# An S4 convolution and SwiGLU block on one core: the front's list of steps written anew, with all its loads in it

## The chip, the core and the metric

The kernel runs on one core of a Trainium2 chip. A core has a matrix engine (TensorE, PE in the profile), a vector engine (VectorE, DVE), a scalar engine (ScalarE, ACT) that evaluates functions from loadable tables, a general engine (GpSimd, POOL), and a sync engine (SyncE, SP) that does nothing but issue DMA transfers. Each engine works through its own instructions in order and waits on semaphores for the others. PE reads from SBUF and writes to PSUM; DMA moves data between DRAM and SBUF. The metric is the device time of one execution in microseconds (us), as the median of several runs.

## The reference

The input `x` has 2048 rows of 640 channels. A conditioning vector `c` gives six modulation rows. The first half is an S4 long convolution, the second a SwiGLU feed-forward net:

```python
mod = (silu(c) @ w_mod).reshape(1, 6, 1, 640)       # sa, ca, ga, sb, cb, gb
h = layernorm(x) * (1 + ca) + sa
dt = exp(log_dt)[:, None]
P = exp((dt * A)[:, :, None] * arange(2048))        # A, B, C complex, 640 x 128
K = einsum("dn,dnl,dn->dl", C, P, dt * B).real      # 640 x 2048
y = irfft(rfft(pad(h)) * rfft(pad(K)))[:2048] + h * Dskip
x = x + ga * y
h = layernorm(x) * (1 + cb) + sb
x = x + gb * ((silu(h @ w1) * (h @ w3)) @ w2)       # w1, w3: 640 x 1728
```

## The kernel before

The kernel has four stretches. The **front** makes everything that the convolution needs to start: the modulation, the normalized input after a first transform stage, and the first part of the convolution's kernel `K`. A **loop** then runs the convolution in five chunks of 128 channels (`NDC`), while it goes on making `K`. A short part turns the result back, and the feed-forward net with its matrix products takes the rest. Only the front, and the first steps of the loop, are touched here.

`K` is made in 40 steps of 16 channels (`NS`, `SD`). For a step, PE multiplies small tables into exponents (`exp_fast`, `exp_slow`: words `PA`, `PQ`), ScalarE takes `Exp` of them (`XA`, `XQ`), POOL makes integer phases in two instructions (`phases`, word `PH`: the product of turns and a ramp, then the addition of a shift to half of it), ScalarE takes the absolute value, cosine and sine of them (`AB`, `CO`, `SI`), VectorE multiplies (`E1`, `E2`, `A1`, `A2`), PE sums products to `pk` (`kg`), VectorE adds and scales (`K`), PE does a first transform stage (`pt`) and ScalarE copies the result into the buffer `uk` (`uk`). `Exp` on one side, and the sine and arctangent on the other, are in different tables, so a change between them costs an `ACT_TABLE_LOAD`.

The front runs the first nine to twelve of these steps, mixed with the rest of its work:

- Parameters: `prm` holds A, B, C, loaded for the first 128 channels (`d0`) and for the other 512 (`d1`). Words `z1` to `zK` turn the first part into the tables that `PA`, `PQ` and `PH` read (`thi` and `phi` are what `PH` reads); words `d0` to `dN` do so for the other 512 channels. `d0` stands on POOL, `d1` on VectorE.
- Modulation: eight column blocks of `w_mod` early (`ms+0` to `ms+7`) and five late (`qs+0` to `qs+4`), each a group of PE matmuls, a VectorE copy (`mp`, `qp`), a PE transposition (`mc`, `qc`) and a VectorE copy into columns (`mv`, `qv`). Five blocks lie in the rooms `wm`, three (`wg`) come into rooms that the first blocks leave, and the five late ones (`wl`) into rooms in `uk` that the parameters leave.
- Input: 16 tiles of 128 rows are loaded (`xl`), measured (`ls`, `lg`, `lv`) and normalized (`ln`). `s1` to `s4` make a row and a `shift` from the modulation. Per tile PE does the first transform stage (`um`), VectorE or ScalarE evicts the two halves with the shift (`ua`, `ub`; `/s` means by ScalarE), and `us` stores the tile to DRAM. `ul` loads that result back, in another layout, into `uk`; four such loads of two DMAs each for a chunk.

Words such as `PA+0/A/3` stand in one long string, `FRONT`. The program walks it from left to right and emits each word's instructions, and every engine keeps the order of its own. The number behind a slash is a count of idle matmuls (`warm`, a product of the identity with itself) that PE does ahead of the word; each is two matmuls in the profile. Some loads of the front stood outside the string: once the words `ms+0`, `ms+1`, `ms+2` were out, a piece of code behind the loop issued the three `wg` blocks, three input tiles and the second part of `prm`, all on SP's queue. When the string ends, the pools `hpz` and `pm_` on the right of SBUF are closed and the pool `fp` opens in their place. `fp` holds the matrices of the second transform stage (`s2`, three buffers) and of the inverse (`i1`).

The first step of the loop is `stage2` for chunk 0 and group 0 (L655 in the profile, `p<-uk,s`): 16 matmuls that need the first `s2` matrices, `ul+0` in `uk` and the front's last `uk` copy. ScalarE's copy `kc` of its result opens VectorE's products.

Of the kernel before, what the change touches and what calls it, by code (L numbers as in the profile page):

```python
# [108 lines left out]
def tile_kernel(ctx: ExitStack, tc: tile.TileContext, a):  # L109
# [248 lines left out]
    pmod, part = {}, {}  # L358

# [17 lines left out]
    def early_sums(i, n):  # L377
        pm = psS.tile([P, 512], F32, name="pm", tag=("pb", "pk")[i % 2 if i < 5 else (i - 5) % 2], bufs=1)
        warm(pm, n)
        mod_sums(i, (wm + wg)[i], pm)  # L380
# [178 lines left out]

    def phases(s):  # L560
        sl = slice(s * SD, s * SD + SD)
        p = tp.tile([P, SD, NPH], I32, name="ph", bufs=4)
        keep(G.tensor_tensor(p, bc(thi[:, sl], 2, NPH), bc(iota, 1, SD), op=OP.mult))  # L563
        keep(G.tensor_tensor(p[:, :, :NA], p[:, :, :NA], bc(phi[:, sl], 2, NA), op=OP.add))  # L564
        ph[s] = p
# [77 lines left out]

    def stage2(ch, g):
        s2 = fp.tile([P, 4, P], F32, name="s2", bufs=3)
        nc.sync.dma_start(s2, a["s2"][:, g * 4:g * 4 + 4, :])
# [176 lines left out]
    def of(p, name, *args):  # L823
        return lambda *n: getattr(p, name)(*args, *n)

    once_parts = {
        "r2": lambda: Vo.tensor_tensor(r2, bc(selx, 2, NB), bc(stepx[:, :NB], 1, NA), op=OP.mult),
# [21 lines left out]
        "xl": ln1_load, "us": u_store, "wl": late_load, "ul": lambda i: u_load(0, i),  # L849
# [39 lines left out]
    for word in FRONT:  # L889
# [739 lines left out]
```

## Time and profile before

| what | value |
|---|---|
| median of 3 runs | 964.46 us (963.45 to 967.33) |
| profiled execution | 967.25 us |
| its span, first to last instruction | 965.5 us |
| mean granted TensorE clock | 0.986 |
| PE busy over the span | 900.3 us (93%) |
| VectorE busy | 709.2 us (73%) |
| ScalarE busy | 560.9 us (58%) |
| POOL busy | 280.9 us (29%) |
| first matmul of the loop (`stage2`) | 153.72 us after the span's start |

Rows of a timeline give start, duration, engine, line, operation, the tiles written and read, and in brackets the engine's idle time before it with what ended that. Rows of stretches give the busy time of PE, PE's weight loads, VectorE, ScalarE and POOL in turn, each with its count of instructions, and then the granted PE clock, the busy share of the DMA engines and GB/s. Nearly all calls in the front go through one recording helper, so their line is L103 for PE and VectorE and L137 or L140 for ScalarE, and the tile's name tells them apart. "SPq" is SP's issuing of DMAs.

### The profile page before, as it was taken

How to read it: one execution, taken by the hardware profiler on the slowest of the kernel's cores; microseconds unless marked ns; L12 is line 12 of the kernel's file. 1: busy time of each engine (PE TensorE's matmuls, PEld its weight loads, DVE VectorE, ACT ScalarE, POOL GpSimd, SP SyncE). 2: the span in 40 equal slices, each digit the busy share in tenths (PEclk: the TensorE clock that was granted, in tenths of full speed). 3: DMA queues.
4: the chain of work that ended last, by engine and by line, in shares of the span. 5: the costliest groups of instructions: out<-in, count | busy, mean ns of one | idle time of the engine just before them, and what ended most of it. 6: DMA issues, size and time to landing. Idle time of an engine off the chain costs nothing.

```text
span 965.5 us, 21228 instructions
## 1 busy us (share of the span) xinstructions
PE 900.3 (93%) x8524; PEld 706.3 (73%) x8524; DVE 709.2 (73%) x1249; ACT 560.9 (58%) x815; POOL 280.9 (29%) x278
## 2 busy tenths in 40 slices
PE   4899996888888899899999999999999999999997
PEld 3676674666666676568888887777888888888886
DVE  6688975999999995677666665686887766664665
ACT  4778986999999964255433333365743333323432
POOL 2623452545564621224322210111422222200000
PEclk8999999999999999799999999999999999999999
DMA  8545598555566799593313114995422221103452
GB/s 250 165 165 192 193 269 203 141 158 134 148 165 160 186 220 277 158 277 130 84 53 109 56 55 116 244 254 178 142 91 82 77 60 52 52 21 98 147 170 103
DMA packets 103720, 140.79 MB, mean 146 GB/s; under 512 B 20581, under 2 KB 62821, under 8 KB 103621
## 3 DMA queue, kind: packets, MB, share of 16 engines
q1 hardware_dynamic: 99812, 129.34, 46.7%
q0 software_dynamic: 2304, 7.74, 2.4%
q10 hardware_dynamic: 1504, 2.36, 0.8%
q8 instruction: 67, 1.10, 0.5%
q14 instruction: 33, 0.26, 0.1%
HBM read 107.94 MB, written 31.46 MB: 144 GB/s over the span
## 4 chain that ended last, share of the span: by engine, by line
PE 80%; ACT 8%; DVE 4%; DMA 3%; issue 3%; SPq 0%; ACTq 0%; POOL 0%; DVEq 0%; POOLq 0%
PE ps L103 56%; PE p L655 6%; PE pu L103 3%; ACT A L137 3%; PE pk L605 3%; PE pt L624 3%; PE pm L103 3%; PE pz L697 2%; ACT cs L137 2%; DMA zs<-zt 2%; PE pa L537 1%; PE pq L548 1%; PE pa L103 1%; PE pT L103 1%; ACT uk L140 1%
## 5 line engine op out<-in xcount | busy, mean ns | idle before, releaser
L103 DVE TENSOR_TENSOR s<-ps,s 128x512 f32<-128x512 f32 x138 | 94.9, 687 | 79.9 <-PE ps L103 79.7
L563 POOL TENSOR_TENSOR ph<-thi,iota 128x1024 int32<-128x1024 int32 x40 | 95.0, 2376 | 138.4 <-DVE A L591 69.5
L103 DVE TENSOR_TENSOR gl<-rw,gh 128x640 fp32r<-128x640 f32 x87 | 78.2, 898 | 64.9 <-ACT gh L103 64.8
L103 ACT CAST gh<-rw 128x640 fp32r<-128x640 f32 x87 | 63.3, 727 | 104.0 <-PE ps L103 62.2
L655 PE MATMUL p<-uk,s 128*64 128x256 f32 x640 | 79.7, 391 | 19.1 <-issue 9.9
L103 PE MATMUL ps<-xA,gh 128*128 128x512 f32 x280 | 87.9, 392 | 0.4 <-ACT xA L103 0.4
L103 PE MATMUL ps<-gh,uh 128*128 128x512 f32 x224 | 87.5, 391 | 0.0
L103 POOL TENSOR_TENSOR S<-rw 128x256 f32<-128x256 f32 x46 | 36.6, 798 | 174.0 <-DVE S0l L103 154.7
L103 PE MATMUL ps<-gl,uh 128*128 128x512 f32 x224 | 87.2, 389 | 0.0
L103 PE MATMUL ps<-gh,ul 128*128 128x512 f32 x208 | 81.1, 390 | 0.0
L655 PEld LDWEIGHTS p<-uk,s 128*64 128x64 f32 x640 | 46.1, 139 | 42.3 <-issue 14.3
L584 DVE TENSOR_TENSOR E<-A,cs 128x1024 f32<-128x1024 f32 x40 | 60.3, 1509 | 1.7 <-ACT cs L137 1.7
L103 PEld LDWEIGHTS ps<-xA,gh 128*128 128x128 f32 x280 | 52.1, 188 | 13.0 <-ACT xA L103 1.0
L103 PE MATMUL ps<-xA,gl 128*128 128x512 f32 x140 | 54.5, 389 | 0.0
L564 POOL TENSOR_TENSOR ph<-ph,phi 128x512 int32<-128x512 int32 x40 | 49.5, 1236 | 6.5 <-DVE phi L103 3.5
L591 DVE TENSOR_TENSOR A<-A,ph 128x1024 f32<-128x1024 f32 x40 | 50.4, 1260 | 0.0
L103 ACT ACTIVATE s<-ps 128x512 f32<-128x512 f32 (+1 forms) x33 | 19.6, 595 | 51.3 <-PE ps L103 51.3
L103 PEld LDWEIGHTS ps<-gl,uh 128*128 128x128 f32 x224 | 42.1, 188 | 9.0
L103 PEld LDWEIGHTS ps<-gh,uh 128*128 128x128 f32 x224 | 42.0, 188 | 8.8
L697 PEld LDWEIGHTS pz<-Y,i 64*128 64x128 f32 x640 | 39.4, 188 | 11.1 <-issue 5.8
L697 PE MATMUL pz<-Y,i 64*128 64x128 f32 x640 | 44.4, 282 | 3.2 <-issue 2.7
L137 ACT ACTIVATE A<-pa 128x1024 f32<-128x1024 f32 x40 | 41.1, 1029 | 8.5 <-PE pa L537 8.2
(241 smaller groups left out, 2318.3 us busy)
## 6 DMA issues: line engine op xcount, KB each, us to landing
rw<-in_w_dram SPq DMA_DIRECT2D x52, 320.0 KB
us<-u SPq DMA_DIRECT2D x16, 640.0 KB
s<-in_s_dram SPq DMA_DIRECT2D x40, 256.0 KB
i<-in_i_dram SPq DMA_DIRECT2D x40, 256.0 KB
rw<-in_wg_dram SPq DMA_DIRECT2D x31, 320.0 KB
rw<-in_wu_dram SPq DMA_DIRECT2D x28, 320.0 KB
uk<-us SPq DMA_DIRECT2D x32, 256.0 KB
zs<-zt SPq DMA_DIRECT2D x32, 256.0 KB
```

Source lines behind the costliest of these rows:

```text
L103: ins = fn(*args, **kw)
L137: return tc.keep_in_program_order(S.activation(*args, **kw))
L140: return tc.keep_in_program_order(S.copy(out, in_))
L537: keep(PE.matmul(pA[s][:, rr, :], la[r, t, :], r2[r, js, :].rearrange("p j b -> p (j b)"), start=True, stop=True, tile_position=(r.start, 0)))
L563: keep(G.tensor_tensor(p, bc(thi[:, sl], 2, NPH), bc(iota, 1, SD), op=OP.mult))
L564: keep(G.tensor_tensor(p[:, :, :NA], p[:, :, :NA], bc(phi[:, sl], 2, NA), op=OP.add))
L584: keep(V.tensor_tensor(EC[s][:, :, 1:3, :], AA[s][:, :, 1:3, :], mid(cs[s]), op=OP.mult))
L591: keep(V.tensor_tensor(A[:, :, 1:3, :], A[:, :, 1:3, :], mid(ph[s]), op=OP.mult))
L605: keep(PE.matmul(pk[dq * 32:dq * 32 + 32, g, :], x[:, g * 4 + dq, 1, :], x[:, g * 4 + dq, 0:3:2, :], start=(st == 0), stop=(st == 1), tile ...
L624: keep(PE.matmul(pt[c * 64:c * 64 + 64, g, :], kk[:, g, :], s1[:, c, :], start=True, stop=True, tile_position=(0, c * 64)))
L655: keep(PE.matmul(p2[par * 64:par * 64 + 64, pi, c, :], s2[:, pi * 2 + par, c * 64:c * 64 + 64], uk[:, 0:kn + 1:kn, f, :], start=True, stop ...
L697: ins = keep(PE.matmul(pz[:, par, (g % 2) * 2 + pi, :], i1[r, pi, c, :], Y[r, pi, c, :], start=(c == 0), stop=(c == 1), tile_position=(par ...
```

## The change

Five things are done:

- The loads that the code behind the loop issued become words of the string: `wg+0` to `wg+2`, `pd` (the second part of `prm`) and `xl+4` to `xl+6`.
- `PH` is split: `PH` keeps the product, and a new word `PI` does the addition of the shift.
- In the pool `pm_` the tiles `lt` and `scb` change their places, so that what lies at the place of the first `s2` buffers is something else.
- The words `ul+1` to `ul+3` leave the string. Behind it the first three `s2` loads are issued at once, in program order, and then the three `ul` loads. `stage2` takes these three `s2` tiles instead of loading its own.
- The string is written in another order, with other counts of idle matmuls (117 in all, where there were 205) and another division of the evictions (17 by ScalarE, where there were 16). ScalarE's order has 19 table loads up to its first `kc`, where it had 18.

```diff
@@ pool pm_
-    scb = pm_.tile([P, KD, NA], F32, name="scb")
     rrow = pm_.tile([P, D], F32, name="rrow")
     shift = pm_.tile([P, D // 2], F32, name="shift")
+    lt = pm_.tile([P, 2, D - DC], F32, name="lt")
+    scb = pm_.tile([P, KD, NA], F32, name="scb")
     cols = pm_.tile([P, 7, KD], F32, name="cols")
-    lt = pm_.tile([P, 2, D - DC], F32, name="lt")
@@ modulation
+    wg = {}
+    def gate_load(i):
+        n = (256, 256, 128)[i]
+        wg[i] = w_load(w_room(1, i, n, 1280), 1280 + 256 * i)
@@ phases
+    def phase_turns(s):
+        p = ph[s] = tp.tile([P, SD, NPH], I32, name="ph", bufs=4)
+        keep(G.tensor_tensor(p, bc(thi[:, s * SD:s * SD + SD], 2, NPH), bc(iota, 1, SD), op=OP.mult))
+    def phase_shift(s):
+        p = ph[s]
+        keep(G.tensor_tensor(p[:, :, :NA], p[:, :, :NA], bc(phi[:, s * SD:s * SD + SD], 2, NA), op=OP.add))
@@ second stage
+    def s2_load(g):
+        s2 = fp.tile([P, 4, P], F32, name="s2", bufs=3)
+        (Qo if len(s2_first) < 3 else nc.sync).dma_start(s2, a["s2"][:, g * 4:g * 4 + 4, :])
+        s2_first.append(s2)
+        return s2
     def stage2(ch, g):
-        s2 = fp.tile([P, 4, P], F32, name="s2", bufs=3)
-        nc.sync.dma_start(s2, a["s2"][:, g * 4:g * 4 + 4, :])
+        s2 = s2_load(g) if ch or g >= 3 else s2_first[g]
@@ once_parts
+        "pd": lambda: Qo.dma_start(prm[:, :, d1], prma[:, :, d1]),
@@ FRONT, its first words
-        "r2 z1 x0 z2 z3 ld2 sc zF sel zG ms+0/1 z4 z6 z5 zB zJ z7 zH r1 zC mp+0 ms+1/1 zI z8 z9/4 mp+1 mc+0 "
+        "r1 r2 x0 sel sc ms+0 z5 z1 z7 z8 xl+4 z2 z9 ld2 z3 ms+1 mp+0 zA zF mc+0 z4 zG zJ PA+0/A/3 z6 mp+1 "
...
@@ the walk through FRONT
-        if not wg and {"ms+0", "ms+1", "ms+2"} <= emitted:
-            wg = [w_load(w_room(1, i, c, 1280), 1280 + 256 * i) for i, c in enumerate((256, 256, 128))]
-            for j in range(4, 7):
-                ln1_load(j)
-            Qo.dma_start(prm[:, :, d1], prma[:, :, d1])
-    in_order[0] = False
     pre.close()
     fp = ssm.enter_context(tc.tile_pool(name="fp", bufs=2, side="right", reuse_waits="tile"))
+    for g in range(3):
+        s2_load(g)
+    for i in range(1, 4):
+        u_load(0, i)
+    in_order[0] = False
```

**SP at the front's end.** Here stand the last late blocks of `w_mod`, the last store `us`, the loads of `uk` from `us` (`ul`), the `s2` and `i1` matrices, before:

```order
L103 DMA us_57<-u_1449 128x1280
L103 DMA uk_82<-in_w_mod_dram 128x5x288
L103 DMA uk_82<-in_w_mod_dram 128x5x96
L103 DMA uk_82<-in_w_mod_dram 128x5x384
L103 DMA uk_82<-us_57 64x8x128 x8
L646 DMA s2_1820<-in_s2_dram 128x512
L646 DMA s2_1889<-in_s2_dram 128x512
L646 DMA s2_1999<-in_s2_dram 128x512
L688 DMA i1_2043<-in_i1_dram 128x512
L688 DMA i1_2158<-in_i1_dram 128x512
L688 DMA i1_2215<-in_i1_dram 128x512
```

and now:

```order
L103 DMA uk_82<-in_w_mod_dram 128x5x384
L103 DMA us_57<-u_1340 128x1280
L103 DMA uk_82<-us_57 64x8x128 x2
L103 DMA s2_1728<-in_s2_dram 128x512
L103 DMA s2_1730<-in_s2_dram 128x512
L103 DMA s2_1732<-in_s2_dram 128x512
L103 DMA uk_82<-us_57 64x8x128 x6
L651 DMA uk_82<-us_57 64x8x128 x2
L705 DMA i1_1959<-in_i1_dram 128x512
L658 DMA s2_2018<-in_s2_dram 128x512
L705 DMA i1_2074<-in_i1_dram 128x512
L658 DMA s2_2110<-in_s2_dram 128x512
```

The first three `s2` loads now stand behind two `uk` loads instead of eight. The last `us` store has moved behind all late blocks of `w_mod`. The first `i1` load has moved behind the two loads for chunk 1, which wait for the second `stage2`.

**SP early on.** Behind the constants and the first four input tiles stood:

```order
L103 DMA uk_82<-in_w_mod_dram 128x5x160
L103 DMA uk_82<-in_w_mod_dram 128x5x96
L103 DMA uk_82<-in_w_mod_dram 128x5x256
L103 DMA uk_82<-in_w_mod_dram 128x5x128
L103 DMA x_286<-in_x_dram 128x640
L103 DMA x_288<-in_x_dram 128x640
L103 DMA x_290<-in_x_dram 128x640
L103 DMA uk_82<-in_prm_dram 128x6x512
```

and now:

```order
L103 DMA x_170<-in_x_dram 128x640
L103 DMA uk_82<-in_w_mod_dram 128x5x160
L103 DMA uk_82<-in_w_mod_dram 128x5x96
L103 DMA uk_82<-in_prm_dram 128x6x512
L103 DMA x_240<-in_x_dram 128x640
L103 DMA uk_82<-in_w_mod_dram 128x5x256
L103 DMA x_345<-in_x_dram 128x640
L103 DMA x_433<-in_x_dram 128x640
L103 DMA uk_82<-in_w_mod_dram 128x5x128
```

The large `prm` load has moved ahead of the second and third `wg` blocks, each of which waits until PE has left its room.

**VectorE ahead of the shift.** `cols` are the modulation's columns; the five instructions with `cols` on both sides are `s1`, whose result PE turns into the row from which the shift is made. Ahead of them stood:

```order
L103 COPY part_351<-pm_342 128x256
L584 TENSOR_TENSOR E_366<-A_242,cs_248 128x16x64
L587 TENSOR_TENSOR E_366<-A_242,cs_248 128x16x32
L103 SCALAR_TENSOR_TENSOR rs1_229<-mv1_228,rs1_229 128x2
L103 COPY part_387<-pm_353 128x256
L103 COPY cols_105<-pm_353 128x2
L103 SCALAR_TENSOR_TENSOR rs1_304<-mv1_303,rs1_304 128x2
L591 TENSOR_TENSOR A_242<-A_242,ph_223 128x16x64
L595 SCALAR_TENSOR_TENSOR A_242<-ph_223,A_242 128x16x32
L103 COPY cols_105<-pm_342 128x2
L103 TENSOR_SCALAR cols_105<-cols_105 128x5 x2
```

and now:

```order
L103 BN_STATS st1_265<-x_136 128x6 x2
L103 BN_AGGR mv1_266<-st1_265 128x2
L103 COPY part_322<-pm_253 128x256
L103 COPY part_326<-pm_307 128x256
L103 BN_STATS st1_328<-x_170 128x6 x2
L103 BN_AGGR mv1_329<-st1_328 128x2
L103 COPY cols_106<-pm_307 128x2
L103 COPY cols_106<-pm_253 128x2
L103 TENSOR_SCALAR cols_106<-cols_106 128x5 x2
```

The four products of step 0 (`E` and `A`) have moved from ahead of `s1` to behind it, and the statistics of a fifth input tile have come ahead of it.

More of the change, by code (lines that the diff above doesn't have):

```diff
@@ L379, in early_sums @@
         warm(pm, n)
-        mod_sums(i, (wm + wg)[i], pm)
+        mod_sums(i, wm[i] if i < 5 else wg[i - 5], pm)
     def early_turn(i):
@@ L558, in slow @@
             pQ.pop(s)[:, :, :256].rearrange("p r (j b) -> p r j b", j=8), AF.Exp)
-    def phases(s):
[L561 to L565, printed above, removed]
+    def phase_turns(s):
[4 more added lines that the diff above has]
+        keep(G.tensor_tensor(p[:, :, :NA], p[:, :, :NA], bc(phi[:, s * SD:s * SD + SD], 2, NA), op=OP.add))
+    def phases(s):
+        phase_turns(s)
+        phase_shift(s)
     def absph(s):
@@ L848, in tile_kernel @@
         "qs": late_sums, "qp": lambda i: mod_part(("l", i)), "qc": late_turn, "qv": late_cols,
[L849 removed]
+        "xl": ln1_load, "us": u_store, "wl": late_load, "wg": gate_load, "ul": lambda i: u_load(0, i),
         "ls": ln_sums, "lg": ln_power, "lv": ln_bias, "ln": ln_apply}
@@ L908, in tile_kernel @@
                 done.add((name, k))
-                if name == "PA":
+                if name == "PH":
+                    phase_turns(k)
+                elif name == "PI":
+                    phase_shift(k)
+                elif name == "PA":
                     exp_fast((k,), tag, n)
```

2 lines of the change are left out of this document (1 added, 1 removed), and 45 rows, old and new, of the table FRONT.

## The prediction

> **What bounds the kernel now.** I read first, in the view of the timeline, how the front hands over to the loop, since the change ends there.
>
> ```profile
> 134.34 11.50 SPq L103 DMA_DIRECT2D uk<-us  x8
> 145.88 2.59 SPq L646 DMA_DIRECT2D s<-in_s_dram  x3
> 148.57 1.62 SPq L688 DMA_DIRECT2D i<-in_i_dram  x3
> 147.85 1.09 PE L624 MATMUL pt<-s,K 128*64 128x128 f32 x16
> 148.99 0.58 ACT L140 COPY uk<-pt 128x512 f32<-128x512 f32 x1 [0.17 <-PE pt L624]
> 153.72 3.56 PE L655 MATMUL p<-uk,s 128*64 128x256 f32 x16 [4.78 <-issue]
> 157.31 0.59 ACT L140 COPY kc<-p 128x512 f32<-128x512 f32 x1 [6.78 <-PE p L655]
> 160.25 1.95 PE L655 MATMUL p<-uk,s 128*64 128x256 f32 x16 [0.91 <-PE pt L624]
> 172.10 1.05 PE L697 MATMUL pz<-Y,i 64*128 64x128 f32 x16
> ```
>
> The first second-stage group could start when ScalarE's last `uk` copy is done, at 148.99 + 0.58 = 149.57. It starts at 153.72. The profile gives "issue" as the reason, which names no engine; what that group still needs is data, and its matrices `s` were issued last, at 145.88, behind eight `uk` loads that kept SP's queue for 11.50 us. PE then runs this group in 3.56 us where the next takes 1.95. ScalarE, whose `kc` copy opens the loop, stands idle for 6.78 us. So the front's end holds about 6 us in which no engine gets on.
>
> Next I read the front in five stretches (busy time of PE, weight loads, VectorE, ScalarE, POOL; clock; DMA share; GB/s).
>
> ```profile
> 0.00:38.00 38.00, 25.19 (x210) 20.61 (x212) 21.73 (x65) 22.90 (x31) 13.95 (x17) 0.91 0.87 263
> 38.00:52.00 14.00, 9.90 (x98) 8.08 (x99) 10.71 (x16) 10.38 (x14) 7.70 (x5) 0.88 0.00 0
> 52.00:75.00 23.00, 22.38 (x313) 17.37 (x313) 20.61 (x36) 17.39 (x24) 9.03 (x14) 1.00 0.53 188
> 75.00:110.00 35.00, 33.52 (x567) 24.39 (x570) 32.16 (x73) 32.02 (x40) 11.48 (x13) 1.00 0.52 189
> 110.00:150.00 40.00, 37.79 (x689) 28.81 (x688) 30.54 (x49) 35.15 (x41) 22.02 (x12) 1.00 0.89 246
> ```
>
> PE looks busiest, but much of that is idle matmuls (below). From 75 to 150 ScalarE works 67.17 of 75 us and is the bound. Ahead of that it is idle 15.10, 3.62 and 5.61 us, 24.3 of 75. The DMA engines rest completely from 38 to 52. Those two facts are what another order can use; the sum is made on ScalarE.
>
> The reasons for the early idle time are in the timeline from 4 to 56 us:
>
> ```profile
> 18.48 9.17 SPq L103 DMA_DIRECT2D uk<-in_w_mod_dram  x4
> 19.29 0.89 DVE L103 BATCH_NORM_STATS2 st<-x 128x6 f32<-128x320 f32 x2 [0.38 <-DMA x<-in_x_dram]
> 20.39 1.02 ACT L137 ACTIVATE A<-pa 128x1024 f32<-128x1024 f32 x1 [0.55 <-PE pa L537]
> 27.25 0.42 DVE L103 COPY part<-pm 128x256 f32<-128x256 f32 x1 [5.81 <-PE pm L103]
> 29.37 0.38 SPq L103 DMA_DIRECT2D uk<-in_prm_dram  x1
> 37.67 4.80 POOL L103 TENSOR_TENSOR uk<-uk 128x512 f32<-128x512 f32 x3 [6.72 <-DMA uk<-in_prm_dram]
> 40.09 1.25 DVE L103 TENSOR_SCALAR cols<-cols 128x5 f32<-128x5 f32 x2
> 44.40 2.50 PE L103 MATMUL pr<-ident,cols 128*128 128x128 f32 x10 [4.10 <-DVE cols L103]
> 46.94 1.06 ACT L137 ACTIVATE shift<-pr,misc 64x320 f32<-64x320 f32 x2 [3.18 <-PE pr L103]
> 55.94 0.69 ACT L140 COPY u<-pu 128x640 f32<-128x640 f32 x1 [3.02 <-PE pu L103]
> ```
>
> SP spends 9.17 us on the four `w_mod` loads, waiting for PE to leave their rooms, and the large `prm` load behind them goes out at 29.37 and lets POOL start at 37.67. VectorE reaches `s1` at 40.09, so PE waits 4.10 us for the columns and the shift is made at 46.94. No input tile can be transformed before.
>
> **The parts of the change.**
>
> *The first `s2` loads ahead of six `uk` loads.* Eight `uk` issues took 11.50 us with their waits, so six of them are 8.6 us of SP's time that no longer stand ahead. The data are then there before the last `uk` copy, and the first group follows that copy. The wait 149.57 to 153.72 goes: 4.15 us. The group's duration goes from 3.56 to 1.95 if PE is not left idle: 1.61. Sum 5.8 us. Seen from ScalarE: of its 6.78 us about one is left, while PE does 1.95 us and ScalarE one more absolute value. The other room in `pm_` costs nothing by itself; it only decides on whom the load waits. What is late next: in the new order the first `i1` load waits behind two loads for chunk 1, and these for the end of the second group. Before, that group began at 160.25 and the inverse at 172.10, 11.85 us apart, against 1.95 for the group and 11.50/8 = 1.4 us for each of two issues ahead; 7 us are left for the `i1` data to land. I cost it at nothing, covered by ScalarE's and VectorE's work between the two. The last `us` store, which `ul+0` needs, has moved behind all late `w_mod` loads:
>
> ```profile
> 125.59 1.18 SPq L103 DMA_DIRECT2D us<-u  x1
> 126.81 4.93 SPq L103 DMA_DIRECT2D uk<-in_w_mod_dram  x3
> ```
>
> On the old clock it would go out at 126.81 + 4.93 = 131.7 instead of 125.59 and land, by my estimate from the 8.3 us that the `prm` load took (29.37 to 37.67), by 140. Then `ul+0` goes out 5.7 us later than 134.34, and its two issues and the first `s2` are out at 143: data at 145 to 149, just ahead of 149.57. So this cover is thin, and with a shorter front the first group may wait for data by some us; I leave this in the range.
>
> *The loads inside the list.* The large `prm` load now waits for one `wg` block and not for three. That lets it go out at about 20 instead of 29.37; it lands by about 28 to 30, since the DMA engines were at full share until 20. POOL's and VectorE's parameter steps come 8 us sooner. On the path this counts only through the next part.
>
> *The new order at the start.* Ahead of `s1` VectorE now has statistics of five tiles, five copies and the phase steps, and no product. From 19.29, when the first tile has landed: five times 1.1 us (0.89 and 0.21 more for the closing step; an estimate), five copies at 0.42, about 2 us of small steps, and `s1`, 4.2 us when it ran beside POOL (40.09 to 44.3) and about 1 alone: it ends between 30 and 33, against 44.3. The wait of 5.81 us falls away, since the third block of sums no longer stands behind eighteen idle words on PE. So the shift is then bound by ScalarE's own order ahead of it, priced by the rows of the front's instructions by form:
>
> ```profile
> L143 ACT ACT_TABLE_LOAD x18 | 23.1, 1283 | 1.5 <-PEq L1618 1.2
> L137 ACT ACTIVATE x<-x,rs 128x640 f32<-128x640 f32 x16 | 14.4, 913 | 0.0
> L137 ACT ACTIVATE cs<-ph 128x1024 f32<-128x1024 int32 x13 | 13.6, 1056 | 0.0
> L137 ACT ACTIVATE cs<-cs,hp 128x1024 f32<-128x1024 f32 x12 | 13.5, 1140 | 0.0
> L137 ACT ACTIVATE A<-pa 128x1024 f32<-128x1024 f32 x12 | 12.3, 1025 | 5.4 <-PE pa L537 5.1
> L140 ACT COPY u<-pu 128x640 f32<-128x640 f32 x16 | 10.8, 688 | 5.8 <-PE pu L103 4.0 <-issue 1.6 <-ACT x L137 0.2
> L137 ACT ACTIVATE A<-pq 128x512 f32<-128x512 f32 x12 | 7.1, 597 | 3.5 <-PE pq L548 3.4
> ```
>
> From the first `A<-pa` on: four of them (4.1), four table loads (5.1), two normalizations (1.8), three absolute values (3.2), two `A<-pq` (1.2), three sines and cosines (3.3), small casts and the arctangent (about 1.6): 20.3 us. The first one came at 20.39; it now needs one flip and one table and no arctangent ahead of it, so 16 to 20. The shift comes at 36 to 41, 6 to 11 us sooner, take 8. But less is done by then: before, ScalarE had worked 22.90 of the first 38 us and some 5.5 up to 46.94, about 28.4; now 20.3 and about 4 ahead, 24.3. That is 4.1 us still to do. One table load (1.28) and one eviction (0.69) are added, 2.0 us. Lead at the shift: 8 - 4.1 - 2.0 = 2 us, with ends 0 and 5. Afterwards 5.61 us of idle time stood between 52 and 75, 3.02 of it waiting for the first evictions. With POOL and VectorE further ahead, I take 4 of the 5.61, ends 0 and 5.6. From 75 to 150 ScalarE was idle 7.8 us; I leave that as it is, ends 2 better and 2 worse. The front's own gain: 2 + 4 = 6 us, from -2 to 12.
>
> *Phases in two parts.* The same two POOL instructions, and by the five stretches POOL works 64 of 150 us. The product no longer waits for the shift's tables. Nothing by itself; what it lets come sooner is in the 20.3 us above.
>
> *Fewer idle matmuls.* They have two rows each in nine groups by tile, the first and the last of them being
>
> ```profile
> L103 PE MATMUL pm<-ident 128*128 128x128 f32 x84 | 13.4, 302 | 7.4 <-DMA ident<-in_ident_dram 7.4
> L103 PE MATMUL pg<-ident 128*128 128x128 f32 x16 | 2.1, 281 | 0.0
> ```
>
> with 410 matmuls in the nine. By these two rows one costs 0.13 to 0.16 us of PE's time, so 88 words fewer are 176 matmuls or 23 to 28 us. They are covered now (ScalarE is the bound), so I cost them at nothing; what they may cost is the clock:
>
> ```profile
> 16.00:18.00 2.00, 0.56 (x4) 0.56 (x4) 1.90 (x7) 0.00 (x0) 0.00 (x0) 0.77 1.08 366
> 22.00:24.00 2.00, 2.00 (x12) 2.00 (x12) 0.00 (x0) 1.97 (x3) 1.96 (x2) 0.53 0.57 98
> 24.00:26.00 2.00, 2.00 (x20) 2.00 (x19) 0.00 (x0) 2.00 (x4) 1.92 (x2) 1.00 1.13 310
> 17.44 0.69 PE L103 MATMUL pT<-ident,uk 128*128 128x128 f32 x2 [2.54 <-DVE uk L103]
> ```
>
> A pause of 2.54 us was enough to bring the granted clock to half, and it took until 24 to come back. One such pause costs PE about 3 us of work. At the start PE is waited for, so by this row the sum would be 3 us smaller for one pause there. [...]
>
> **The sum.** 5.8 + 6 = 11.8 us: the profiled execution would go from 967.25 (span 965.5) to 955.4. It stood 2.8 above the median of 964.46; taken off the median, 952.7 us.
>
> **Rivals.**
> 1. *The front gives its gain back*: ScalarE's idle time returns elsewhere, as waits for PE and DMA, because the list was made for durations that do not come. Only the 5.8 us stay: 958.7. For it: the later stretches have little idle time to lose and 2 us of work are added. Against it: the early loads and the early shift do not hang on fine timing.
> 2. *Slower, by a cold PE*: with 176 matmuls fewer PE pauses often, and the clock stays at half. PE's 128.8 us of the front become about 103, in 141 us a share of 0.73; at half clock L us of front need 1.46 L. It eats the 11.8 us at L = 26 and is 0.5% slower from L = 36. If it is cold from 52 to 110, 58 us, it loses 26.7: 979. Against it: from 52 on the clock was 1.00, and pauses there were short.
> 3. *The wait isn't moved*: `ul+0` behind the late `us` store, or something else that the profile calls "issue", holds the first group as long as before, and the front's gain is lost in that wait: about 964.
>
> **Chances.** The forecast 0.70, rival 1 0.15, rival 2 0.08, rival 3 0.07. The forecast's own ends are 5.8 - 2 = 3.8 and 5.8 + 12 = 17.8 us, so 946.7 to 960.7, which holds rival 1 too. I give 947 to 961. A change of 0.5%, 4.8 us, is about what a measurement can tell from none, so faster means under 959.6: the forecast and two thirds of rival 1, 0.80. Within 0.5%: the rest of rival 1 and most of rival 3, 0.11. Slower: rival 2 and a little, 0.09.
>
> **What would show it.** Right: `p<-uk,s` begins within a microsecond of the last `uk<-pt` and takes about 2 us; it lies near 141 to 149; POOL's wait for `prm` ends near 29; the shift's row lies near 38; ScalarE is idle less than 20 of the first 75 us. Wrong: an "issue" wait of several us ahead of `p<-uk,s`; clocks of 0.5 in stretches between 30 and 110; new ScalarE waits of 2 us and more behind 75; a wait of the first `pz` for its matrices.

## The result and the profile after

| | before | after |
|---|---|---|
| median | 964.83 us (963.45 to 967.33) | 955.08 us (953.06 to 957.20) |
| ratio | | 0.9896, 95% interval 0.9867 to 0.9926 |
| profiled execution, its span | 967.25 us, 965.5 us | 957.20 us, 955.4 us |
| mean granted clock | 0.986 | 0.983 |

The change made the kernel 9.75 us faster by the medians; 11.8 us were forecast. The medians are of four executions each. They scatter by some us, and the experiments show part of the reason.

The front's end first. This is the timeline after, SP's issues above and the two engines below, for comparison with the first block of the prediction.

```profile
126.13 1.40 SPq L103 DMA_DIRECT2D us<-u  x1
134.83 1.30 SPq L103 DMA_DIRECT2D uk<-us  x2
136.18 1.57 SPq L103 DMA_DIRECT2D s<-in_s_dram  x3
137.85 7.17 SPq L103 DMA_DIRECT2D uk<-us  x6
146.12 0.56 ACT L140 COPY uk<-pt 128x512 f32<-128x512 f32 x1
146.73 1.95 PE L672 MATMUL p<-uk,s 128*64 128x256 f32 x16 [0.99 <-ACT uk L140]
148.72 0.59 ACT L140 COPY kc<-p 128x512 f32<-128x512 f32 x1 [1.09 <-PE p L672]
163.51 1.05 PE L714 MATMUL pz<-Y,i 64*128 64x128 f32 x16
```

The three `s2` issues stand at 136.18 and no longer behind all the `uk` loads. The first group starts 0.05 us after the last copy (146.12 + 0.56 = 146.68), takes 1.95 us instead of 3.56, and ScalarE waits 1.09 us instead of 6.78. The first `pz` (the matmuls of the inverse) has no wait. The `kc` copy comes 157.31 - 148.72 = 8.6 us sooner. The spans differ by 10.1; from that copy to the span's end it took 808.2 us before and 806.7 after, and between 805.0 and 809.3 in the experiments' profiles, so the last 1.5 us aren't shown to be the change's.

Of the 8.6 us, 4.1 are the wait that stood ahead of the first group (153.72 - 149.57, now 0.05), 1.6 the group's own duration, and 2.9 the front (149.57 to 146.68). So the handover gave what was forecast, 5.8, and the front less than half of its 6. Where that went is in the five stretches after (PE, weight loads, VectorE, ScalarE, POOL, clock, DMA share, GB/s):

```profile
0.00:38.00 38.00, 24.52 (x177) 16.55 (x177) 25.09 (x78) 23.21 (x33) 15.86 (x19) 0.97 0.82 254
38.00:52.00 14.00, 11.44 (x94) 6.39 (x94) 11.90 (x20) 12.26 (x16) 9.04 (x12) 0.50 0.49 166
52.00:75.00 23.00, 20.99 (x300) 15.34 (x308) 19.39 (x39) 22.49 (x26) 6.96 (x9) 0.77 0.44 160
75.00:110.00 35.00, 31.55 (x548) 22.65 (x540) 26.12 (x56) 29.39 (x38) 12.06 (x9) 0.95 0.42 151
110.00:146.68 36.68, 34.86 (x606) 25.93 (x590) 26.41 (x45) 31.83 (x38) 17.76 (x11) 1.00 0.94 271
```

ScalarE is idle 14.79, 1.74 and 0.51 us in the first 75, together 17.0 instead of 24.3: 7.3 less. From 75 to the last copy it is idle 5.61 + 4.85 = 10.5 instead of 7.8: 2.6 more. It does 119.2 us of work instead of 117.4: 1.8 more. 7.3 - 2.6 - 1.8 = 2.9, the front's gain to the tenth. So the early part came, and later idle time took a third of it back.

The third figure from the right, the clock, has changed most: 0.50 from 38 to 52 and 0.77 from 52 to 75, where it was 0.88 and 1.00. The rows early on, in order of time:

```profile
23.98 0.59 SPq L103 DMA_DIRECT2D uk<-in_prm_dram  x1
32.78 3.83 POOL L103 TENSOR_TENSOR uk<-uk 128x512 f32<-128x512 f32 x3 [4.74 <-DMA uk<-in_prm_dram]
33.59 0.89 DVE L103 BATCH_NORM_STATS2 st<-x 128x6 f32<-128x320 f32 x2 [3.60 <-DMA x<-in_x_dram]
35.67 1.01 PE L103 MATMUL pm<-misc,part 128*128 128x1 f32 x4 [2.75 <-DVE part L103]
39.63 1.06 ACT L137 ACTIVATE shift<-pr,misc 64x320 f32<-64x320 f32 x2 [3.11 <-PE pq L553]
```

`prm` goes out 5.4 us sooner and POOL starts 4.9 us sooner, at 32.78. VectorE has a new wait of 3.60 us for the input tile whose load now stands behind `prm`; PE pauses 2.75 us for VectorE's copy (32.92 to 35.67), and the clock falls at 35.46. The shift is at 39.63 instead of 46.94.

### The profile page after: what moved, and what is told of

Same layout as the page of the kernel before. It is cut to its first block, busy times and chain, and to the rows that moved or that the text cites. A ratio compares the mean times of both kernels' runs of the same rounds, so it can differ in the third digit from the quotient of the medians.

```text
span 955.4 us, 20892 instructions
## 1 busy us (share of the span) xinstructions
PE 890.0 (93%) x8356; PEld 691.6 (72%) x8356; DVE 702.9 (74%) x1248; ACT 562.5 (59%) x817; POOL 278.7 (29%) x278
## 3 DMA queue, kind: packets, MB, share of 16 engines
q10 hardware_dynamic: 1504, 2.36, 0.8%
## 4 chain that ended last, share of the span: by engine, by line
PE 73%; ACT 10%; DMA 3%; issue 3%; DVE 2%; ACTq 0%; SPq 0%; POOL 0%; DVEq 0%; POOLq 0%
PE ps L103 55%; PE p L672 6%; ACT A L137 3%; PE pz L714 3%; DMA zs<-zt 2%; PE pt L634 2%; ACT cs L137 2%; PE pk L615 2%; PE pq L553 1%; PE pa L542 1%; ACT uk L140 1%; PE pm L103 1%; ACT ph L137 1%; PE pq L103 1%; PE pu L103 1%
## 5 line engine op out<-in xcount | busy, mean ns | idle before, releaser
L567 POOL TENSOR_TENSOR ph<-thi,iota 128x1024 int32<-128x1024 int32 x40 | 92.9, 2324 | 146.9 <-DVE A L601 64.5
```

What stands on the lines that cost most here:

```text
L567: keep(G.tensor_tensor(p, bc(thi[:, s * SD:s * SD + SD], 2, NPH), bc(iota, 1, SD), op=OP.mult))
```

## The experiments

Three theories stood at the start. The first is the prediction's: the `s2` loads are worth 5.8 us by themselves, and the new order with its early loads makes the rest. The second: the clock at half, which now lasts from 35.5 to 59.4 us, took back what is missing. The third: the fewer idle matmuls, which the prediction costed at nothing, are what moved the front. All kernels compute the whole reference.

**The handover alone, and the list alone.** The old list with the early `s2` loads:

```diff
 # the kernel before
+    s2_load(0..2) at once when the list ends, then ul+1 to ul+3
-    ... ul+1, ul+2, ul+3 in FRONT; s2 loaded in stage2
+    lt ahead of scb in pm_
```

> The kernel before with its own list, and of the change only this: the first three `s2` loads stand ahead of six `uk` loads, and `lt` and `scb` change places. Theory 1 (the wait at the front's end was for the `s2` data, and it is worth its 5.8 us whatever the front does): 5.8 us less than the kernel before, about 959.0; the wait of 4.78 us ahead of the first `p<-uk,s` falls below 1 us and the group takes 1.95 us. Theory 2 (the wait only fell away because the new list lets SP come to these loads sooner; with the old list something else is as late): less than 2 us of gain, about 964, and an issue wait of 3 to 5 us stays. Theory 3 (the data are early, but the loop after it gives the time back, since ScalarE and VectorE have a fixed amount to do up to the inverse): the group starts sooner and the first `pz` does not; 962 to 965.

and the new list with late ones:

```diff
 # the changed kernel
-    for g in range(3): s2_load(g)
     for i in range(1, 4): u_load(0, i)
+    for g in range(3): s2_load(g)
```

> The changed kernel, with its three first `s2` loads put behind the six `uk` loads, where they stood before; nothing else differs. Theory 1 (5.8 us are the loads', and the new list by itself is worth some 3 to 4 us): SP would come to `s2` at 143.3 and, as the kernel before needed about 7 us from there to the first group, that group starts at about 150.5 to 151.5 and takes longer than 1.95 us: 5 to 6 us more than the changed kernel, 960 to 961. Theory 2 (the two parts need each other): the whole gain goes, 964 or more. Theory 3 (the new list is worth more by itself, since the shorter front only moved the wait): 957 to 958.

Measured: the old list with early `s2` 960.17 us beside 965.31 before, ratio 0.9937 (0.9913 to 0.9960), 5.1 us less. The new list with late `s2` 962.00, ratio 0.9963 (0.9943 to 0.9983), 3.3 us less than before and 6.9 more than the changed kernel. The profiled execution of the first is its slowest of nine (968.15 us), that of the second its fastest of ten (958.79), so their rows are read for the wait and not for the time. The first of the two, in its timeline:

```profile
141.09 2.50 SPq L103 DMA_DIRECT2D s<-in_s_dram  x3
154.40 0.59 ACT L140 COPY uk<-pt 128x512 f32<-128x512 f32 x1 [0.17 <-PE pt L624]
155.04 1.95 PE L662 MATMUL p<-uk,s 128*64 128x256 f32 x16 [0.68 <-ACT uk L140]
```

and the second:

```profile
136.88 2.11 SPq L103 DMA_DIRECT2D s<-in_s_dram  x3
141.75 0.56 ACT L140 COPY uk<-pt 128x512 f32<-128x512 f32 x1
145.60 3.28 PE L672 MATMUL p<-uk,s 128*64 128x256 f32 x16 [4.24 <-issue]
148.92 0.59 ACT L140 COPY kc<-p 128x512 f32<-128x512 f32 x1 [5.65 <-PE p L672]
```

The wait follows the place of the `s2` loads with either list: none with early ones, 4.24 us and a slow group of 3.28 with late ones. That is theory 1 of both expectations, with times about 1 us above what each named; the times speak against a gain that needs the new list, or one that the loop gives back. The second also shows how long the data take: 145.60 - 136.88 = 8.7 us from the first issue, 7.8 in the profile before (145.88 to 153.72). By that estimate the data of the changed kernel were there at about 144 to 145, one to three us ahead of the last copy. The cover is as thin as the prediction said.

The second profile holds a surprise: with the very list of the changed kernel its last `uk` copy ends at 142.31, 4.4 us sooner than in the profile after. The old list does the like: its last copy ended at 149.57 in the profile before and at 154.99 in the kernel with early `s2`, whose edit touches only the loads at the list's end and the places of two tiles. So the front of one list differs by 4 to 5 us from one execution to another.

**The same kernel again.**

> The changed kernel once more, for a second profile and more times. Theory 1 (the granted clock falls for whole spans of 3.4 us, whose phase against the program differs from execution to execution, so that one and the same pause of PE costs the clock in one execution and not in another): the dips behind 62 us are not at 69.6 and 83.2 as in the first profile, but elsewhere or absent; the last `uk<-pt` copy ends at 142 to 144 us with none of them and at 145 to 148 with two or more; the median is 954 to 957. Theory 2 (the dips belong to the order and come each time): they stand within a microsecond of the same places, and the last copy ends at 146 to 147.

955.75 us (951.48 to 959.54, six executions), ratio 0.9890 (0.9864 to 0.9915). Its profile, the stretches from 38 and the handover:

```profile
38.00:52.00 14.00, 10.77 (x92) 5.94 (x92) 11.90 (x19) 12.94 (x17) 8.36 (x11) 1.00 0.49 166
52.00:75.00 23.00, 21.67 (x340) 15.76 (x340) 20.92 (x48) 22.76 (x27) 6.97 (x9) 1.00 0.50 173
75.00:110.00 35.00, 31.54 (x544) 22.75 (x541) 27.61 (x52) 31.53 (x42) 12.92 (x10) 1.00 0.47 172
```

```profile
142.32 0.56 ACT L140 COPY uk<-pt 128x512 f32<-128x512 f32 x1
144.93 0.59 ACT L140 COPY kc<-p 128x512 f32<-128x512 f32 x1 [1.09 <-PE p L672]
```

Here the clock never falls ahead of the loop. The last copy ends at 142.88, and `kc` comes 157.31 - 144.93 = 12.4 us sooner than before: 6.7 for the front and 5.7 for the handover. The profile after fell twice behind 62 us:

```profile
68.00:70.00 2.00, 1.56 (x28) 1.20 (x36) 1.93 (x6) 1.97 (x3) 1.37 (x2) 0.90 0.80 305
70.00:72.00 2.00, 2.00 (x23) 0.98 (x8) 1.15 (x5) 1.67 (x3) 0.59 (x2) 0.50 0.47 182
72.00:74.00 2.00, 2.00 (x69) 1.73 (x68) 0.39 (x1) 2.00 (x3) 0.30 (x1) 0.75 0.54 164
82.00:84.00 2.00, 1.78 (x9) 1.43 (x10) 0.00 (x0) 1.97 (x3) 0.29 (x1) 0.81 1.03 426
84.00:86.00 2.00, 2.00 (x48) 1.78 (x50) 0.00 (x0) 2.00 (x3) 0.00 (x0) 0.50 0.61 253
86.00:88.00 2.00, 2.00 (x54) 1.45 (x50) 1.06 (x4) 0.35 (x1) 0.00 (x0) 0.83 0.03 8
```

Worked out from the shares, it is half from 69.6 to 73 and from 83.2 to 86.7. That is theory 1: the same program, other places or none. In each of the thirteen profiles with a fall ahead of 160 us, the falls last 3.4 us or a multiple, up to 23.9, and lie on one grid of that step; where the grid begins differs between executions (the edges are in the last section).

**The clock, from 36 to 60.** Eight idle words fill PE's pause:

```diff
-    ... SI+0 s2 mp+5 ...
+    ... SI+0 s2/8 mp+5 ...
```

> The changed kernel with eight idle words (16 matmuls) ahead of the transposition in `s2`, as the old list had them, so that PE does not pause from 33 to 35.7. Theory 1 (the clock of 0.50 from 36 to 58 costs time): the granted clock there is 0.8 to 1.0, and the time falls; if PE set the pace there it would be by up to 0.46 of 20 us, 9 us; if it is in the way now and then, by 1 to 3 us. Theory 2 (ScalarE sets the pace there, 34.8 of 37 us busy from 38 to 75, so a cold PE costs nothing): the clock rises and the time stays within 0.7 us. Theory 3 (the pause is not what lowers the clock): the clock stays at 0.50 and the time too.

The clock from 38 to 52 rose from 0.50 to 0.76, a little less than theory 1 asked for:

```profile
38.00:52.00 14.00, 8.02 (x90) 4.20 (x88) 12.49 (x22) 12.60 (x17) 8.71 (x11) 0.76 0.51 166
```

and the median is 954.63 (953.39 to 964.44), within 0.5 us of the changed kernel. Its last copy ends at 143.23. With late `s2` loads, where the clock was 0.50 from 36.8 to 60.7, it ended at 142.31, and in the second profile of the changed kernel, where the clock did not fall ahead of the loop, at 142.88. So half clock ahead of 60 costs the front nothing that shows: theory 2.

**An early stall, and the phases.** `ls+5` behind `s3`:

```diff
-    ... s1 ls+5 lv+1 ... s3 s4 um+0/A ...
+    ... s1 lv+1 ... s3 ls+5 s4 um+0/A ...
```

> The changed kernel with the word `ls+5` (statistics of the sixth input tile) moved from behind `s1` to behind `s3`. In the changed kernel VectorE waits there 3.60 us for that tile, whose load stands behind the large `prm` load. Theory 1 (that wait holds VectorE's copies, through them PE and the shift, and so the front): the wait of 3.60 us goes, PE's pause of 2.75 us at 33 to 35.7 shrinks, the row of the shift comes 2 to 3 us sooner than 39.63, and the time falls by 1.5 to 3 us, to 952 to 953.5. Theory 2 (from 75 us on ScalarE waits for PE and not for what comes early, so an earlier shift only makes a longer wait there): the shift comes sooner and the time stays within 0.7 us of the changed kernel.

The shift came at 37.51, 2.1 us sooner, and the median is 955.00, 0.1 us from the changed kernel's. That fits theory 2, an early shift that buys nothing, but doesn't prove it: in this profile the clock was at half from 100 to 113.6, and the last copy ended at 147.27.

```diff
-    ... PH+0 mc+1 PH+1 ... PI+1 ms+4 PI+0 ...
+    ... mc+1 ... PH+1 PI+1 ms+4 PH+0 PI+0 ...   (and so for all thirteen)
```

> The changed kernel with the phases whole again: each product stands right ahead of its addition, where the addition stands now. The prediction's step (the split by itself costs and brings nothing): within 1 us of the changed kernel, 954 to 957. Theory 2 (the product done early is what lets ScalarE's first absolute values come early): the first `ph<-ph` of ScalarE comes 1.5 to 4 us later, the shift too, and the time rises by 1 to 3 us. Theory 3 (the split costs POOL time between its other steps): 1 us faster.

The first `ph<-ph` came at 36.96 instead of 32.53, the shift at 40.84 instead of 39.63, and the median is 956.21, within 1 us of the changed kernel. The split by itself is worth nothing that shows, as forecast.

Six profiles now have the new list with its 117 words or nearly so (the changed kernel twice, late `s2`, the eight words more, `ls+5` later, the whole phases). In the three in which the clock did not fall between 62 us and the last copy, that copy ends at 142.3 to 143.2. In the three with two, three and four steps of 3.4 us at half clock there, it ends at 146.7, 149.2 and 147.3. So what the clock does behind 62 us is worth some 4 to 6 us of the front with this list, and differs between executions.

**The idle matmuls.** First more and fewer of them in the new list.

```diff
 # the changed kernel; 31 words of PE between um+2 and um+15 with one idle word more each
-    ... um+2/A ... PQ+2/A ... kg+0/5 ...
+    ... um+2/A/1 ... PQ+2/A/1 ... kg+0/6 ...
```

> The changed kernel with one idle word more ahead of each of 31 words of PE between `um+2` and `um+15`: 148 words instead of 117, 62 matmuls, 8 to 10 us of PE, some of it in pauses. Theory 1 (dips behind 62 us are what separates a front that ends at 142 to 143 from one that ends at 147, and more idle matmuls prevent them): no dip behind 62 us, the last copy ends at 143 to 144, and the time is 952 to 954. Theory 2 (PE has no room for them, 31.5 of the 35 us from 75 to 110 being busy): ScalarE's waits for PE grow by 2 to 4 us and the time is 957 to 959, dips or none.

```diff
 # the changed kernel, every count left out
-    ... PA+0/A/3 ... kg+0/5 ... PQ+4/A/11 ...
+    ... PA+0/A ... kg+0 ... PQ+4/A ...
```

> The changed kernel without any of its 117 idle words, so 234 matmuls fewer. By the rows of idle matmuls (0.13 to 0.16 us each) that is 30 to 37 us of PE. Theory 1 (they keep the clock up, and a clock at half behind 62 us costs ScalarE waiting time): more than 15 us between 62 and 140 at a clock of 0.50, the last `uk<-pt` copy ends at 148 or later, and the time is 958 to 965. Theory 2 (they stand in the way of real work and keep nothing): the dips are no more than in the changed kernel, ScalarE waits 1 to 3 us less, and the time is 952 to 954.

With 148 words: 959.77 us, ratio 0.9938 (0.9917 to 0.9959), 4.0 us more than the changed kernel beside it, though the clock did not fall between 61 and the loop. With none: 956.05, the same as with 117. The stretch from 75 to 110 of the two, 148 words first:

```profile
75.00:110.00 35.00, 32.13 (x538) 23.77 (x540) 26.04 (x55) 28.59 (x37) 11.81 (x10) 1.00 0.45 162
```

```profile
75.00:110.00 35.00, 28.77 (x448) 17.30 (x442) 27.75 (x56) 28.86 (x38) 11.02 (x9) 0.60 0.44 163
```

With 148 words ScalarE works 28.59 us at full clock, where in the profile of the changed kernel without a fall it worked 31.53: PE has no room for more, theory 2, at a price just above its range. Without any the clock is 0.60 and ScalarE works as much, 28.86. The time lies between the ranges of its two theories, and each had one half right: without idle matmuls the clock fell (37.6 us at half between 62 us and the last copy, beside 6.8 and none in the two profiles of the changed kernel), and the PE time saved paid for it.

If 31 words more cost 4 us, the 88 words that the change left out of the old list need not have been free. So the old list, with its order, its loads and its late `s2`:

```diff
 # the kernel before; every count times 117/205
-    ... ms+2/10 ... PA+2/A/12 ... um+2/A/10 ...
+    ... the same words in the same order, 117 idle words in all
```

> The kernel before with 117 idle words instead of 205: every count of its own list scaled down alike; its order, its loads and its `s2` are as they were. Theory 1 (the idle matmuls of the old list stood in the way of real work, as the 31 words added to the new list did, and the new list's gain by itself is mostly their absence): 23 to 28 us of PE less bring 3 to 5 us, 960.5 to 962.5. Theory 2 (they were covered, as the prediction has it, and the new order and the early loads make the gain): within 1 us of the kernel before, 964.5 to 966.5. Theory 3 (they kept the clock): slower by 1 us or more.

```diff
 # the kernel before, every count left out
-    ... ms+2/10 ... PA+2/A/12 ... um+2/A/10 ...
+    ... ms+2 ... PA+2/A ... um+2/A ...
```

> The kernel before with none of its 205 idle words. In the new list leaving out all 117 changed nothing that the times can tell (956.05 beside 955.75), because some 38 us at half clock paid for the work saved. Theory 1 (idle words stood in the way in the old list): 960 to 963. Theory 2 (covered): 964 to 967, with 30 us and more at a clock of 0.50 behind 50 us. Theory 3 (the clock decides): 968 and more.

| kernel | idle words | `s2` | median, us | profiled execution, us | its last `uk` copy ends |
|---|---|---|---|---|---|
| before | 205 | late | 965.3 | 967.25 | 149.57 |
| old list | 205 | early | 960.17 | 968.15 | 154.99 |
| old list | 117 | late | 961.05 | 961.47 | 141.73 |
| old list | 0 | late | 954.57 | 951.55 | 141.02 |
| new list | 117 | late | 962.00 | 958.79 | 142.31 |
| changed kernel | 117 | early | 955.08 | 957.20 | 146.68 |
| changed kernel again | 117 | early | 955.75 | 955.15 | 142.88 |
| new list | 148 | early | 959.77 | 959.10 | 150.25 |
| new list | 0 | early | 956.05 | 956.05 | 146.22 |

(The last two columns are of one execution each. Between 62 us and the last copy the clock was at half for 13.7 us in the second row's, 10.2 in the third's, 38.8 in the fourth's, 6.8 in the first of the changed kernel's and 37.6 in the last row's, and not at all in the other four.)

With the counts trimmed to 117 the old list took 961.05 us, ratio 0.9945 (0.9927 to 0.9962), 4.2 us less than before. That is theory 1, and it is what the new list with late `s2` took, 962.00. Its rows, the stretches and then the timeline:

```profile
0.00:38.00 38.00, 23.71 (x194) 19.17 (x194) 24.38 (x74) 25.26 (x35) 15.50 (x17) 1.00 0.85 263
38.00:52.00 14.00, 10.57 (x140) 7.44 (x146) 10.92 (x19) 10.91 (x15) 9.08 (x7) 0.88 0.12 48
52.00:75.00 23.00, 19.84 (x252) 13.55 (x252) 21.38 (x44) 20.64 (x27) 8.54 (x14) 0.85 0.60 198
```

```profile
35.25 0.37 DVE L103 TENSOR_SCALAR cols<-cols 128x5 f32<-128x5 f32 x2
37.43 3.45 POOL L103 TENSOR_TENSOR uk<-uk 128x512 f32<-128x512 f32 x2 [5.52 <-DMA uk<-in_prm_dram]
40.81 1.04 ACT L137 ACTIVATE shift<-pr,misc 64x320 f32<-64x320 f32 x2
141.16 0.57 ACT L140 COPY uk<-pt 128x512 f32<-128x512 f32 x1
147.22 3.27 PE L655 MATMUL p<-uk,s 128*64 128x256 f32 x16 [6.44 <-issue]
```

ScalarE's idle time in the first 75 us is 12.74 + 3.09 + 2.36 = 18.2, so 6.1 of the 7.3 us that the new list saved there come with fewer idle matmuls alone. `s1` is reached at 35.25 instead of 40.09 and the shift made at 40.81 instead of 46.94, with `prm` as late as ever (POOL at 37.43). The last copy ends 7.8 us sooner than in the profile before, more than the 4 to 5 us by which the front of one list differed between two executions. Then the old wait takes part of it back: 6.44 us for the `s2` data and a group of 3.27.

Without any idle word the old list took 954.57, ratio 0.9879 (0.9858 to 0.9900), as fast as the whole change. Here even the late `s2` loads fit:

```profile
52.00:75.00 23.00, 20.07 (x301) 11.01 (x300) 22.59 (x50) 22.16 (x30) 9.50 (x16) 0.61 0.61 216
75.00:110.00 35.00, 30.23 (x512) 18.81 (x512) 33.20 (x55) 32.12 (x39) 16.32 (x12) 0.71 0.56 202
```

```profile
132.62 1.99 SPq L646 DMA_DIRECT2D s<-in_s_dram  x3
141.07 1.95 PE L655 MATMUL p<-uk,s 128*64 128x256 f32 x16 [0.68 <-ACT uk L140]
```

They go out at 132.62 instead of 145.88, and the group starts 8.45 us later, about when data and copy are both there. The expectation had no theory that reached this low; a clock of 0.61 and 0.71 over these 58 us (52 to 110) cost less than the 205 idle words with which the profile before has 1.00 in both stretches.

Two last ones search for the best count in the new list:

```diff
 # the changed kernel, every count halved: 59 words
-    ... PA+0/A/3 ... kg+0/5 ... PQ+4/A/11 ...
+    ... PA+0/A/2 ... the same words in the same order
```

> The changed kernel with 59 idle words instead of 117, every count halved. With 148 it took 959.8, with 117 about 955.5, with none 956.1. Theory 1 (a flat bottom: each idle matmul left out saves PE time and costs clock in like measure): 955 to 956.5. Theory 2 (the best count lies between): 953 to 954.5.

```diff
-    ... kg+2/4 ua+7 ... PQ+7/B/7 E1+4 ...
+    ... kg+2 ua+7 ... PQ+7/B E1+4 ...
```

> The changed kernel without the 11 idle words ahead of `kg+2` and `PQ+7`, which took 1.93 and 1.83 us of PE at 83.1 and 88.4 in the profile after, while ScalarE waited 2.24 us for a `pu` and 1.42 us for a `pq`. Theory 1 (the idle matmuls themselves make ScalarE wait there): 1.5 to 3 us less than the changed kernel, 952.5 to 954. Theory 2 (only the clock of 0.50 in that execution made them long): no change beyond 0.7 us in the median, and in a profile without a dip there the two waits are below 1 us with or without them.

954.78 (ratio 0.9889, 0.9863 to 0.9914) and 953.63 (0.9865, 0.9843 to 0.9888). The first lies between the ranges of its two theories, 0.2 us from the flat bottom of theory 1 and 0.3 from theory 2, so it tells only that halving the count costs nothing. Its last copy ended at 143.92 although the clock was at half for 13.7 us behind 62: in this one execution the falls cost less than in the six profiles above. The second has the lowest median of all, some 1.5 us below the changed kernel's first, but its interval overlaps theirs: in the time a hint for theory 1 and not a proof.

The profiles go further. ScalarE's row for `PQ+7` in the second profile of the changed kernel, where the clock did not fall ahead of the loop, and then without the 11 words:

```profile
86.90 0.60 ACT L137 ACTIVATE A<-pq 128x512 f32<-128x512 f32 x1 [1.42 <-PE pq L553]
```

```profile
87.88 0.62 ACT L137 ACTIVATE A<-pq 128x512 f32<-128x512 f32 x1
```

The clock was 1.00 there in both. The wait of 1.42 us is there at full clock and goes with the words: for it theory 1 holds. The wait for the `pu` was 2.24 us in the profile after and only 0.67 at full clock, so most of that one belonged to the fall, as in theory 2.

## Why the prediction was right, and where its reasons were wrong

The time, 955.08, lies in the range of 947 to 961 and 2.4 us above the 952.7 forecast; it is faster, as forecast. For the handover it is right for its reasons. For the front the size came out although a term that was put at nothing turned out, in the old list, to be worth about as much as the whole new front gives, so there the number was met by luck. The steps one by one:

- *The first `s2` loads: 5.8 us.* Right in mechanism and size. The wait went, the group took 1.95, and the two experiments on it gave 5.1 and 6.9. The words "if PE is not left idle" were the point: in all three profiles with the wait the group took 3.3 to 3.6 us, and the clock was at half for most of it (153.6 to 157.0 in the profile before, 146.1 to 149.5 in the new list with late `s2`, 143.1 to 150.0 in the trimmed old one).
- *The last `us` store, "this cover is thin".* Right that it is thin, but the working was too kind: by the 7.8 us from the first issue to the group in the profile before, `s2` loads out at 143 would have let the group start at 150 to 151, behind the old last copy, and not at 145 to 149. It held because the store went out at 126.13 instead of 131.7 and `ul+0` at 134.83 instead of 140, so that the data had an estimated one to three us to spare.
- *`i1` behind two loads for chunk 1, nothing.* Right, no `pz` waits.
- *`prm` at about 20, landed by 28 to 30.* Wrong in size: out at 23.98, and POOL started at 32.78, 4.9 us sooner instead of 8. SP stood 3.93 us on an input tile's load ahead of it. The new wait of VectorE behind it wasn't foreseen.
- *`s1` done at 30 to 33, shift at 36 to 41.* Right as numbers: 29.99 and 39.63. The five instructions of `s1` took 1.0 us (28.98 to 29.99) while POOL was idle, where they had taken 4.2 beside POOL; that part is as argued. The cause given for the rest, order and early loads, isn't shown. The trimmed old list made the shift at 40.81 in the old order and without one early load; all that it lost was idle matmuls, also ahead of the modulation's sums. The prediction saw the row (the third block "stood behind eighteen idle words on PE") and did not price it.
- *The front's own gain, 6 us.* Right in size for an execution whose clock does not fall behind 62 us (6.7), 2.9 in the profile after. The term "75 to 150 ... idle 7.8 us; I leave that as it is" failed there by 2.6 us.
- *Fewer idle matmuls: "covered now ... so I cost them at nothing".* This is the step that was wrong. By themselves they bring 4.2 us in the old list, and 7.8 at its last copy in one profile of each. That is as much as the new list brings without the `s2` move (3.3). So the order and the early loads, on which the 6 us were argued, are not shown to bring anything; nor are they shown to be useless, since the trimmed counts don't stand where the new list has its own. The reasoning went from "ScalarE is the bound" to "PE time is free"; but ScalarE waited for PE in the first 75 us, where the trimming alone took 6.1 us off its idle time, and later too: the wait of 1.42 us for `PQ+7` went with the words ahead of it.
- *Phases in two parts, nothing.* Right within the 1 us that the test could tell.
- *Rival 2, a cold PE.* Its sign came: half clock from 35.5 to 59.4 in the profile after, 24 us. Its price, 0.46 us per us, did not hold there: those 24 us cost nothing that shows. Behind 62 us it was not far off: 6.8 us at half clock would cost 3.1, and the front was 3.8 longer. The price took PE's time to count alike in all of the front.
- *Rivals 1 and 3.* The group followed the last copy within 0.05 us, so the wait was moved, against rival 3. Rival 1 came in part: of the front's gain 2.6 us returned as idle time behind 75, with a wait of 2.24 us, one of the signs named for being wrong; in the execution without a fall the front kept 6.7.
- *"One pause costs PE about 3 us of work".* The sum left these 3 us out. The falls of these profiles last 3.4 us or a multiple, so by an estimate from half the clock PE loses 1.7 us of work or a multiple. The pause of 2.54 us in the profile before goes with two steps at half (17.07 to 23.90), the one of 2.75 us after with seven (35.46 to 59.35), and pauses of 0.98 and 1.23 us with one step each in one execution (from 69.59 and 83.25) and with none in the next.
- *The profile's own time, taken off the median.* The profile before stood above its median and had no fall between 48 and 150; the one after was at half until 59.4 and fell twice more. A single profile on each side hid 3.8 of the 12.4 us.

Left open: what sets off a fall of the clock, whether the old list with trimmed counts and early `s2` would reach the changed kernel or pass it, and how much the 11 words ahead of `kg+2` and `PQ+7` cost in the time.

## What to carry to other kernels

An idle matmul is work like any other to whoever stands behind it on PE: here 88 words fewer brought 4.2 us in the old list, and 31 more cost 4.0 in the new one. Price idle matmuls by the waits that they precede, not by the bound of the whole stretch, and try a kernel without them before reordering it. When a change reorders and thins at once, run the thinning alone. Compare two profiles only after looking at where each one's clock fell, since for one program, the changed kernel, it was at half for 30.7 us ahead of the loop in one profile and not at all in the next.

## What the runs showed of the hardware

In these profiles the granted clock stands at 1.00 or 0.50, and its changes lie on a grid. In the profile after it falls at 35.46, 69.59 and 83.25 us: the distances are 34.13 and 13.66, ten and four times 3.413, and the falls last 23.89, 3.42 and 3.41 us, seven, one and one such steps, read from shares of 0.2 us. Its first edges, and the edges of the longest fall behind 62 in the kernel with `ls+5` later (99.97 to 113.62, four steps):

```profile
34.00:36.00 2.00, 0.33 (x2) 0.33 (x2) 1.97 (x6) 1.97 (x3) 1.92 (x3) 0.86 0.36 132
58.00:60.00 2.00, 2.00 (x65) 1.77 (x68) 1.97 (x5) 1.99 (x2) 1.39 (x3) 0.66 0.00 0
```

```profile
98.00:100.00 2.00, 2.00 (x58) 1.21 (x62) 1.24 (x4) 2.00 (x4) 2.00 (x2) 0.99 0.69 284
110.00:112.00 2.00, 2.00 (x18) 1.66 (x17) 0.44 (x1) 2.00 (x4) 2.00 (x1) 0.50 0.07 30
112.00:114.00 2.00, 2.00 (x14) 1.79 (x11) 0.00 (x0) 2.00 (x3) 1.92 (x3) 0.60 0.99 317
```

The thirteen profiles with a fall ahead of 160 us agree on the step: their 46 falls last 3.41 to 23.90 us, one to seven steps, each within 0.02. In four experiments a fall between 383 and 397 lies on the grid of the early ones (383.21, 388.40, 396.82 and 396.92). Where the grid begins, counted from the span's start, is another in each: 0.01 us past a multiple of 3.413 in the profile before and 1.33 in the one after.

PE's busy time in the step ahead does not tell whether the clock falls. PE was busy 2.08 of the 3.4 us ahead of the fall at 99.97, and 3.11 ahead of one at 50.7 in the kernel with 148 words; in the new list without idle words a stretch of one step with 1.19 us of busy time (20.84 to 24.25) kept the full clock. Nor does the clock come back whenever PE is busy for a step: from 100 to 112 PE was busy throughout, at 0.50 (the last 2 us of it are shown).

One pause shows the same. In both profiles of the changed kernel PE pauses 0.98 us for the same ScalarE copy. The step that ends with the fall at 69.59 in the profile after, and then a stretch of 3.42 us in the second, each with that pause in it:

```profile
66.18:69.59 3.41, 2.43 (x40) 1.48 (x36) 2.66 (x7) 3.39 (x4) 3.19 (x2) 1.00 0.43 138
```

```profile
65.10:68.52 3.42, 2.44 (x36) 1.36 (x32) 2.51 (x7) 3.40 (x5) 3.02 (x2) 1.00 0.35 92
```

Behind the first the clock was at half for 3.4 us; behind the second it stayed at 1.00 up to the loop. So PE's busy time is not what tells the two apart; what does, these runs don't show.
